# Gates kept as columns and sent through DRAM, LN2 transposed by DMA, attention DMAs issued by GpSimd, and idle products at the start: a fused attention and feed-forward block

## Chip, cores, metric

One core of a Trainium2 chip. The time is the device time of one execution in microseconds (us); most executions agree within 0.3% for the kernel before. Each experiment was timed in the same rounds, on the same chip, as the kernel before. TensorE is PE, VectorE DVE, ScalarE ACT, GpSimd POOL, SyncE SP.

## The reference

A transformer block on 2048 tokens of width 512, conditioned by a vector c: local attention (32 heads of 16, window of 8 keys at a distance of 2), then a SwiGLU feed-forward part (FFN) of width 1792. All arrays are bf16.

```python
mod = (silu(c) @ w_mod).reshape(1, 6, 1, 512)
sa, ca, ga, sb, cb, gb = ...                  # six rows of 512
h = layernorm(x) * (1 + ca) + sa              # LN1
x = x + ga * attention(h, wqkv, wo)           # ga: a gate on the columns of wo
h = layernorm(x) * (1 + cb) + sb              # LN2
x = x + gb * (silu(h @ w1) * (h @ w3)) @ w2   # gb: a gate on the columns of w2
```

The gates ga and gb are multiplied into wo and w2 once, so each gate has to stand in SBUF as a row of 512 that is repeated on all 128 partitions.

## The kernel before

The kernel is a list of operations with a cost in nanoseconds, an engine and a key. A planner inside the program places them: at each moment it takes, for each free engine, the ready operation of lowest priority number. So the order on each engine follows from the costs, the modelled latencies and a table of tuned priorities. The chip then runs each engine's instructions strictly in that order, with semaphore waits between engines.

```python
LAT = {"sp": 1900, "pe": 230, "dve": 70, "act": 150, "pool": 120}
DMA_RATE = 350
...                                     # in schedule(): how long a DMA takes in the plan
                if o.dma:
                    dma_free = max(busy[e], dma_free) + o.bytes // DMA_RATE
                    o.end = dma_free + LAT["sp"]
```

The gate, with silu(c) spread over 128 equal columns beforehand (`csb`), comes out of PE already repeated on all partitions:

```python
    def gate(i):
        def mm(e):
            for t in range(KT):
                ins = e.matmul(bank(vm), csb[:, t, :], wm_g[i][:, t, :], start=(t == 0), stop=(t == KT - 1))
            return ins
        p.op("pe", mm, 4 * MM, k, r=[vwmg[i], vcsb] + wm_hold, w=[vm])
        p.op("act", lambda e: e.activation(dst[:], bank(vm), ACT.Copy), c_act(512), k, r=[vm], w=[vg[i]])
```

LN2 (and LN1) of a tile of 128 tokens: statistics on DVE, two small GpSimd steps for the reciprocal root, normalisation on DVE, four 128x128 transposes on PE, eviction with scale and shift on ACT:

```python
        vn = Val("xn", xnpool)
        p.op("dve", lambda e: e.tensor_scalar(vn.at[:], x_sb[:, T, :], mv[:, i, 0:1], rs[:, i, :], op0=ALU.subtract,
                                              op1=ALU.mult), 350, ("nm", i), r=[vx[T], vr, vm], w=[vn])
...                                     # ln_T
                p.op("pe", tr, 120, k, r=[vns[tt], vident], part=[vt])
```

The attention weights of a tile go to DRAM and come back in another layout, both issued by SP; then DVE multiplies them with the values (`av`, 128x4096) and PE reduces:

```python
        p.dma(bass.AP(a_dram, ...), ..., ("ad", T), 65536, r=[va, ve], w=[vad], cost=400)
        p.dma(lambda: val.at[:], bass.AP(a_dram, ...), ("al", T), 65536 * 3, r=[vad], w=[val], cost=400)
```

The softmax here doesn't subtract the row's maximum and nothing guards it: scores larger than these inputs give would overflow.

Of the kernel before, what the change touches and what calls it, by code (L numbers as in the profile page):

```python
# [11 lines left out]
P = 128  # L12
# [71 lines left out]
class Program:  # L84
# [41 lines left out]
    def dma(self, out, in_, key, nbytes, r=(), w=(), part=(), after=(), eng="sp", cost=450, group=None):  # L126
        nc = self.nc

        def fn(e):
            a = out() if callable(out) else out  # L130
            b = in_() if callable(in_) else in_
            with nc.allow_non_contiguous_dma(reason="layout"):
                return e.dma_start(a, b)

        o = self.op(eng, fn, cost, key, r=r, w=w, part=part, after=after, dma=nbytes)
        if group is not None:
            group.append(o)
            o.group = group
        return o

    def schedule(self, prio):
# [21 lines left out]
        dma_free = 0  # L163
# [3 lines left out]
        while len(self.placed) < len(ops):  # L167
# [10 lines left out]
            for e in ENGINES:  # L178
# [31 lines left out]
                if o.dma:  # L210
                    dma_free = max(busy[e], dma_free) + o.bytes // DMA_RATE
                    o.end = dma_free + LAT["sp"]
                else:
                    o.end = busy[e] + LAT[e]
# [115 lines left out]
VG = 2  # L330
LN1 = [[0, 1], [2, 3], [4, 5, 6, 7], [8, 9, 10, 11], [12, 13, 14, 15]]
# [3 lines left out]
def _build(p, A_x, A_wqkv, A_wo, B_w1, B_w3, B_w2, c, w_mod, out):  # L335
# [37 lines left out]
    cst = sb([P, 2], f32, "cst")  # L373
# [3 lines left out]
    cT = sb([P, KT], bf, "cT")  # L377
    thc = sb([P, KT], f32, "thc")
    csT = sb([P, KT], f32, "csT")
    csT_bf = sb([P, KT], bf, "csT_bf")  # L380
    modc_bf = sb([P, 16], bf, "modc_bf")
    modc = sb([P, 16], f32, "modc")
# [11 lines left out]
    csb = at([P, KT, P], bf, "csb", 24576)  # L394
    zrow = at([PAD, D], bf, "zrow", 25600)
    wm_g = [at([P, KT, 512], bf, f"wm_g{i}", 12288 * i + 8192) for i in range(2)]
    vsh_x = nc.alloc_sbuf_tensor_at("sb_vshx", [P, 8, D], bf, offset=nc.lookup_mloc(wqkv).addr)

    v_dram = nc.dram_tensor("v_scratch_dram", (PAD + S, D), bf)
    a_dram = nc.dram_tensor("a_scratch_dram", (S, W * H), bf)  # L400
# [19 lines left out]
    def held(pool, items):  # L420

        vals = []
        for i, item in enumerate(items):
# [9 lines left out]
    k = ("const", 0)  # L433
    p.op("pool", lambda e: e.memset(ident[:], 0.0), 150, k, w=[vident])
# [3 lines left out]
    p.op("pool", lambda e: e.memset(cst[:, 1:2], -0.5), 80, k, part=[vcst])  # L438
    k = ("const", 1)
    p.op("pool", lambda e: e.memset(ones[:], 1.0), 150, k, w=[vc])  # L440
# [21 lines left out]
    p.dma(bass.AP(cT, 0, [[KT, P], [1, KT]]), bass.AP(c.tensor, c.offset, [[1, P], [P, KT]]), ("load", 0), 1024, w=[vcT],  # L462
          eng="act")
    for T in range(4):
        p.dma(x_sb[:, T, :], x_view[:, T, :], ("load", 1 if T < 2 else 19), 131072, w=[vx[T]])
    p.dma(wm_s[0][:], wm_view[:, :, 0:1024], ("load", 2), 1048576, w=[vwms[0]])
# [20 lines left out]
    for g in range(NG):  # L487
# [10 lines left out]
    vthc, vcs, vcsb, vcsf = Val("thc"), Val("cs"), Val("csb"), Val("csf")  # L498
    k = ("mod", 0)
    p.op("act", lambda e: e.activation(thc[:], cT[:], ACT.Tanh, scale=0.5), 200, k, r=[vcT], w=[vthc], table="exp")  # L500
    p.op("dve", lambda e: e.scalar_tensor_tensor(csT_bf[:], thc[:], 1.0, cT[:], op0=ALU.add, op1=ALU.mult), 180, k,
         r=[vthc, vcT], w=[vcs])
    p.op("dve", lambda e: e.tensor_scalar(csT_bf[:], csT_bf[:], 0.5, None, op0=ALU.mult), 180, k, w=[vcs])
    k = ("mod", 1)
    p.op("dve", lambda e: e.tensor_copy(csT[:], csT_bf[:]), 180, k, r=[vcs], w=[vcsf])
    for t in range(KT):
        p.op("dve", lambda e, t=t: e.tensor_scalar(csb[:, t, :], ones[:], csT[:, t:t + 1], None, op0=ALU.mult), 180, k,
             r=[vc, vcsf], part=[vcsb])
# [4 lines left out]
    def modulation(i):  # L513
# [12 lines left out]
        p.op("pe", mm, 1000, k, r=[vwms[i], vcs] + wm_hold, w=[vm])  # L526
# [4 lines left out]
        p.op("dve", lambda e: e.tensor_copy(modc[:, jlo:jlo + 8], modc_bf[:, jlo:jlo + 8]), 180, k, r=[vb16], w=[vmod[i]])  # L531

    def gate(i):
        k = ("mod", 4 + i)
        vm = Val("ps_gate", psum)

        def mm(e):
            for t in range(KT):
                ins = e.matmul(bank(vm), csb[:, t, :], wm_g[i][:, t, :], start=(t == 0), stop=(t == KT - 1))
            return ins  # L540

        p.op("pe", mm, 4 * MM, k, r=[vwmg[i], vcsb] + wm_hold, w=[vm])
        dst = (ga_bc, gb_bc)[i]
        p.op("act", lambda e: e.activation(dst[:], bank(vm), ACT.Copy), c_act(512), k, r=[vm], w=[vg[i]])

    def ln_stats(which, T):
# [10 lines left out]
        vn = Val("xn", xnpool)  # L557
        p.op("dve", lambda e: e.tensor_scalar(vn.at[:], x_sb[:, T, :], mv[:, i, 0:1], rs[:, i, :], op0=ALU.subtract,  # L558
# [3 lines left out]
    def ln_T(which, gi, vns):  # L562
        vh = Val("h", hpool)
        n = len(vns)
        for half in range(2):
# [12 lines left out]
            for j in range(2):  # L578
# [14 lines left out]
                if half and not which and gi < 2:  # L593
# [121 lines left out]
    def values(T, i, ve, va):  # L715
# [4 lines left out]
              lambda: ve.at[0][:, i].rearrange("p w h -> p (w h)"), ("ad", T), 65536, r=[va, ve], w=[vad], cost=400)  # L720
        p.dma(lambda: val.at[:], bass.AP(a_dram, T * P * W * H, [[H, P], [16 * W * H, 8], [1, H]]), ("al", T), 65536 * 3,
              r=[vad], w=[val], cost=400)
# [41 lines left out]
    def ffn_unit(gi, n, fi, vh):  # L764
# [11 lines left out]
        p.op("pe", lambda e: mm(e, vgp, w1), 4 * c_mm(n), k, r=[vh, vw13[g]], w=[vgp])  # L776
        p.op("act", lambda e: e.activation(vt.at[:, 0:n], bank(vgp)[:, 0:n], ACT.Silu), c_act(n), k, r=[vgp], w=[vt],  # L777
             table="silu")
        p.op("pe", lambda e: mm(e, vup, w3), 4 * c_mm(n), k, r=[vh, vw13[g]], w=[vup])
# [4 lines left out]
    finals = []  # L784

    def ffn_w2(T, tt, vhh):
        vz = Val("ps_z", psum)
        o = None
        for q in range(2):
            def mm(e, q=q):  # L790
# [5 lines left out]
            o = p.op("pe", mm, 7 * MM, ("z", 2 * T + q), r=vhh[7 * q:7 * q + 7] + [vw2s], part=[vz], after=[o] if q else [])  # L796
        vo = Val("o", opool)
        p.op("dve", lambda e: e.tensor_tensor(vo.at[:], bank(vz), x_sb[:, T, :], ALU.add), c_dve(512), ("zo", T),  # L798
             r=[vz, vx[T]], w=[vo])
        finals.append(p.dma(out2d[T * P:(T + 1) * P, :], lambda: vo.at[:], ("zo", T), 131072, r=[vo], cost=400))  # L800

    modulation(0)
# [24 lines left out]
    for gi, Ts in enumerate(FFN):  # L827
        vns = [ln_stats(1, T) for T in Ts]
        vh = ln_T(1, gi, vns)
        vhh = [ffn_unit(gi, len(Ts) * P, fi, vh) for fi in range(NF)]  # L830
        for tt, T in enumerate(Ts):
            ffn_w2(T, tt, vhh)
# [6 lines left out]
def _priorities():  # L839

    return {
        "ac": [-200350, -305143, -144949, -247454, -248998, -144926, 118091, 153034, 127660, 128134, 144119, -511708, -511789, 144159, 233884,
            140161],
        "ad": [-17874, -30405, -32779, -22500, -24840, -32434, -28265, -27668, 1469, -27769, 384, 367, 2705, 132755, -1479, -1613],
        "al": [-26059, -18199, -29495, -32976, -260310, -30646, -28356, -25679, -27023, -29130, 662, 915, 2008, 137184, 1131, 135573],
        "av": [-237126, -167739, 117729, 116760, 129499, 127502, -3576, 163212, 134914, 166331, 224073, 159673, 234283, 170474, 234369, 175760],
        "const": [-318511, -250028],
        "ex": [-152588, -142436, -140021, 53300, -139876, 74900, 96361, 96500, 96599, 118100, 127701, 139700, 124737, 182900, 182900, 182900],
        "f": [-13079, -234848, -103997, -152504, -114086, -145296, -116384, -248184, -248481, -146619, -145234, -198977, 121830, -31495, -146237,
# [61 lines left out]
```

## Time and profile before

| | kernel before |
|---|---|
| time, median | 255.9 us (255.0 to 256.3) |
| profiled execution | span 253.2 us |
| PE busy | 239.0 us, 94% |
| TensorE clock full from | 16.28 us, to the end |

Three more rows of the before page matter; each has 40 slices of the span, here of 6.3 us. PEclk is the granted TensorE clock in tenths (it takes off only what a record of half rate covers; in this trace the first record, full rate, begins at 16.28 us, so the slower start doesn't show in it), DMA the busy share of the 16 DMA engines, GB/s what they moved.

```profile
PEclk9999999999999999999999999999999999999999
DMA  6997999899954595322369145393001000000101
GB/s 193 359 324 189 293 350 331 210 331 284 241 123 140 142 310 196 64 31 62 106 194 295 54 104 85 87 310 103 4 0 44 0 0 21 21 3 21 41 23 41
```

The view of DMA issues (what, how many, size of each, median us from issue to landing):

```profile
v_scratch_dram<-sb_v SPq DMA_DIRECT2D x16, 128.0 KB, 5.0
a_scratch_dram<-sb_attn SPq DMA_DIRECT2D x16, 64.0 KB, 2.5
```

### The profile page before, as it was taken

To read this page: it belongs to the slowest core of one execution; us is meant where nothing else is said; L and a number is where in the kernel's file an instruction comes from. 1 tells how busy PE (TensorE), PEld (TensorE's weight loads), DVE (VectorE), ACT (ScalarE), POOL (GpSimd) and SP (SyncE) were. 2 spreads that over 40 slices of the span, in tenths; PEclk is the share of its full clock that TensorE was granted. 3 is DMA by queue.
4 is the path that set the end of the run, shared out by engine and by line. 5 is a ranking of instruction groups with operands and counts; after the bars stand their busy time and mean duration, and the time that the engine had idled before them with its cause. 6 is when DMAs were issued, how large, how long until landed. Compare 5 with 4: busy or idle time off the path is not lost.

```text
span 253.2 us, 5473 instructions
## 1 busy us (share of the span) xinstructions
PE 239.0 (94%) x2262; PEld 140.4 (55%) x2296; DVE 191.7 (76%) x298; ACT 111.4 (44%) x198; POOL 32.0 (13%) x81
## 2 busy tenths in 40 slices
PE   0599989999999999999999999999999999999995
PEld 0367555655488666546654544556544444565562
DVE  4759889999998989999899899999952443432432
ACT  2159748864863347432462273334234322420120
POOL 6237641001000040000002200020030000000000
PEclk9999999999999999999999999999999999999999
DMA  6997999899954595322369145393001000000101
GB/s 193 359 324 189 293 350 331 210 331 284 241 123 140 142 310 196 64 31 62 106 194 295 54 104 85 87 310 103 4 0 44 0 0 21 21 3 21 41 23 41
DMA packets 45817, 36.29 MB, mean 143 GB/s; under 512 B 19408, under 2 KB 36576, under 8 KB 45792
## 3 DMA queue, kind: packets, MB, share of 16 engines
q1 hardware_dynamic: 45264, 35.94, 49.4%
q8 instruction: 18, 0.29, 0.5%
q10 hardware_dynamic: 528, 0.00, 0.1%
q14 instruction: 7, 0.06, 0.1%
HBM read 30.67 MB, written 5.26 MB: 142 GB/s over the span
## 4 chain that ended last, share of the span: by engine, by line
PE 87%; DVE 5%; DMA 2%; POOL 2%; issue 1%; SPq 0%; ACT 0%; DVEq 0%
PE pall L771 36%; PE pall L792 19%; PE pall L615 9%; PE pall L755 5%; PE pall L742 5%; PE pall L633 5%; PE pall L673 4%; PE pall L574 2%; DMA sb_x<-in_A_x_dram 2%; POOL sb_rs L555 1%; DVE sb_xn L558 1%; DVE sb_st L550 1%; POOL sb_rs L553 1%; DVE sb_pq L664 1%; DVE sb_hh L780 1%
## 5 line engine op out<-in xcount | busy, mean ns | idle before, releaser
L771 PE MATMUL pall<-sb_h,sb_w 128*128 128x512 bf16 (+1 forms) x548 | 100.0, 336 | 0.7
L771 PEld LDWEIGHTS pall<-sb_h,sb_w 128*128 128x128 bf16 x560 | 53.7, 97 | 41.4
L777 ACT ACTIVATE sb_sg<-pall 128x512 bf16<-128x512 f32 (+1 forms) x70 | 35.6, 511 | 70.6 <-PE pall L771 70.3
L780 DVE TENSOR_TENSOR sb_hh<-sb_sg,pall 128x512 bf16<-128x512 bf16 (+1 forms) x70 | 39.5, 577 | 26.0 <-PE pall L771 23.8
L792 PE MATMUL pall<-sb_w,sb_hh 128*128 128x512 bf16 x216 | 49.7, 379 | 0.4
L664 DVE TENSOR_TENSOR sb_pq<-sb_q,sb_kT 128x4096 bf16<-128x4096 bf16 x16 | 36.4, 2283 | 0.5 <-ACT sb_q L622 0.3
L792 PEld LDWEIGHTS pall<-sb_w,sb_hh 128*128 128x128 bf16 x224 | 21.4, 98 | 23.5 <-DVE sb_hh L780 0.2
L615 PE MATMUL pall<-sb_h,sb_wqkv 128*128 128x512 bf16 (+1 forms) x155 | 31.9, 344 | 0.3
L582 ACT ACTIVATE sb_h<-pall,sb_modc 128x512 bf16<-128x512 bf16 (+1 forms) x36 | 23.1, 708 | 18.7 <-PE pall L574 13.1
L553 POOL TENSOR_TENSOR sb_rs<-sb_mv,sb_cst 128x1 f32<-128x1 f32 x32 | 8.8, 276 | 151.4 <-DVE sb_mv L551 148.4
L733 DVE TENSOR_TENSOR sb_vsh<-sb_vsh,sb_al 128x4096 bf16<-128x4096 bf16 x12 | 27.3, 2285 | 0.4 <-DMA sb_vsh<-v_scratch_dram 0.4
L798 DVE TENSOR_TENSOR sb_o<-pall,sb_x 128x512 bf16<-128x512 f32 x16 | 11.0, 688 | 18.0 <-PE pall L792 18.0
L550 DVE BATCH_NORM_STATS2 sb_st<-sb_x 128x6 f32<-128x512 bf16 x32 | 21.8, 682 | 3.3 <-DMA sb_x<-in_A_x_dram 3.2
L555 POOL TENSOR_TENSOR sb_rs<-sb_rs,sb_cst 128x1 f32<-128x1 f32 x32 | 20.9, 654 | 2.5
L615 PEld LDWEIGHTS pall<-sb_h,sb_wqkv 128*128 128x128 bf16 x160 | 15.1, 101 | 11.0 <-ACT sb_h L582 0.7
L633 PE MATMUL pall<-sb_wqkv,sb_h 128*128 128x512 bf16 x63 | 17.6, 411 | 1.5 <-DVE sb_xn L558 1.3
L574 PE MATMUL pall<-sb_ident,sb_xn 128*128 128x128 bf16 x128 | 12.8, 227 | 6.4 <-DVE sb_xn L558 6.4
L673 PEld LDWEIGHTS pall<-sb_E,sb_pq 128*128 128x128 bf16 x512 | 14.7, 96 | 2.7 <-DVE sb_pq L664 0.6
L748 ACT ACTIVATE sb_ot<-pall 128x512 bf16<-128x512 f32 x16 | 9.6, 598 | 13.6 <-PE pall L742 13.6
L574 PEld LDWEIGHTS pall<-sb_ident,sb_xn 128*128 128x128 bf16 x128 | 9.5, 101 | 10.6 <-DVE sb_xn L558 6.9
L755 PE MATMUL pall<-sb_wo,sb_ot 128*128 128x512 bf16 x58 | 15.0, 379 | 0.3
L673 PE MATMUL pall<-sb_E,sb_pq 128*128 128x32 bf16 x512 | 15.1, 177 | 0.0
(59 smaller groups left out, 163.8 us busy)
## 6 DMA issues: line engine op xcount, KB each, us to landing
sb_vsh<-v_scratch_dram SPq DMA_DIRECT2D x48, 256.0 KB, 4.4
sb_vshx<-v_scratch_dram SPq DMA_DIRECT2D x16, 256.0 KB, 4.5
sb_wm_s<-in_w_mod_dram SPq DMA_DIRECT2D x2, 1024.0 KB, 6.6
v_scratch_dram<-sb_v SPq DMA_DIRECT2D x16, 128.0 KB, 5.0
sb_w<-in_B_w_dram SPq DMA_DIRECT2D x4, 512.0 KB, 7.9
out_dram<-sb_o SPq DMA_DIRECT2D x16, 128.0 KB, 1.7
sb_w<-in_B_w_dram SPq DMA_DIRECT2D x1, 1792.0 KB, 8.9
sb_wqkv<-in_A_wqkv_dram SPq DMA_DIRECT2D x3, 512.0 KB, 7.9
```

The source lines that it names most:

```text
L550: o = p.op("dve", lambda e: e.bn_stats(st[:, i, :], x_sb[:, T, :]), 670, k, r=[vx[T]], w=[vs])
L574: ins = e.transpose(b[:, col:col + P], vns[tt].at[:, ft * P:(ft + 1) * P], ident[:])
L615: ins = e.matmul(bank(vp)[:, 0:n], wqkv[:, t, col:col + P], vh.at[:, t, 0:n], start=(t == 0), stop=(t == KT - 1))
L633: ins = e.matmul(bank(vp), vh.at[:, t, tt * P:(tt + 1) * P], wqkv[:, t, 2 * D:3 * D], start=(t == 0), stop=(t == KT - 1))
L664: return e.tensor_tensor(vp.at[:], in0, in1, ALU.mult)
L673: ins = e.matmul(b[:, c0:c0 + H], vp.at[:, w, ft, :], E_sb[:, ft, :], start=(ft == 0), stop=(ft == KT - 1))
L733: return e.tensor_tensor(v_w, v_w, a_w, ALU.mult)
L755: ins = e.matmul(bank(vy), vt.at[:, ft, :], wo[:, ft, :], start=(ft == 0), stop=(ft == KT - 1))
L771: ins = e.matmul(bank(vp)[:, 0:n], wt[:, t, fi * P:(fi + 1) * P], vh.at[:, t, 0:n], start=(t == 0), stop=(t == KT - 1))
L777: p.op("act", lambda e: e.activation(vt.at[:, 0:n], bank(vgp)[:, 0:n], ACT.Silu), c_act(n), k, r=[vgp], w=[vt], table="silu")
L780: p.op("dve", lambda e: e.tensor_tensor(vh_.at[:, 0:n], vt.at[:, 0:n], bank(vup)[:, 0:n], ALU.mult), c_dve(n), k, r=[vt, vup], w=[vh_])
L792: ins = e.matmul(bank(vz), vhh[fi].at[:, tt * P:(tt + 1) * P], w2[:, fi, :], start=(fi == 0), stop=(fi == NF - 1))
```

## The change

The intent: PE is the bound, so take work from it and start it at full clock. Gates are computed as columns (32 products of one column) and turned into repeated rows by a store to DRAM and a broadcast load; LN2's transposes move from PE to the DMA transpose, its normalisation from DVE to ACT; GpSimd issues the attention DMAs; 80 products of ones keep PE busy before and just behind the first modulation; c is loaded in rows; the last two tiles end in column halves. FFN products get extra dependencies on earlier ones, and all priorities are new.

```diff
+    def warm(i, after=()):
+            for _ in range(4):
+                ins = e.matmul(bank(vw)[:, 0:P], ones[:], ones[:], start=True, stop=True)
...
     def gate(i):
-                ins = e.matmul(bank(vm), csb[:, t, :], wm_g[i][:, t, :], start=(t == 0), stop=(t == KT - 1))
+            for j in range(4):
+                for t in range(KT):
+                    ins = e.matmul(b[:, j:j + 1], wm_g[i][:, t, j * P:(j + 1) * P], csT_bf[:, t:t + 1], ...)
...
+        p.op("dve", lambda e: e.tensor_copy(gcol[:, 4 * i:4 * i + 4], bank(vm)[:, 0:4]), 180, k, r=[vm], w=[vgc])
+        p.dma(bass.AP(g_dram, i * D, [[1, P], [P, KT]]), bass.AP(gcol, 4 * i, [[8, P], [1, 4]]), k, 90000, ..., eng="pool", cost=900)
-        p.op("act", lambda e: e.activation(dst[:], bank(vm), ACT.Copy), c_act(512), k, r=[vm], w=[vg[i]])
+        p.dma(dst[:], bass.AP(g_dram, i * D, [[0, P], [1, D]]), k, 131072, r=[vgd], w=[vg[i]], eng="pool", cost=900)
...
     def ln_stats(which, T):
+        if which:                       # nb = -mean * rstd, two more GpSimd steps
+            p.op("act", lambda e: e.activation(vn.at[:], x_sb[:, T, :], ACT.Identity, bias=nb[:, T, :], scale=rs[:, i, :]), ...)
...
     def ln_T(which, gi, vns):
+        if which and gi >= DMA_T:       # DMA_T = 1: all groups but the first
+                p.dma(lambda tt=tt: vh.at[:, :, tt * P:(tt + 1) * P], lambda tt=tt: vns[tt].at[:], k, 157000, ..., transpose=True)
...
-              ..., ("ad", T), 65536, r=[va, ve], w=[vad], cost=400)
+              ..., ("ad", T), 65536, r=[va, ve], w=[vad], cost=900, eng="pool")
...
     # the planner
-                    dma_free = max(busy[e], dma_free) + o.bytes // DMA_RATE
-                    o.end = dma_free + LAT["sp"]
+                    if e == "sp":
+                        dma_free = max(busy[e], dma_free) + o.bytes // DMA_RATE
+                        o.end = dma_free + LAT["sp"]
+                    else:
+                        o.end = busy[e] + 2 * o.bytes // DMA_RATE + LAT["sp"]
```

The store's destination `[[1, P], [P, KT]]` names element p + 128 t for partition p and column t.

## The prediction

> **What bounds the kernel now.** I read the page's busy shares first, then the slices, the chain that ended last, the waits of the TensorE alone, the timeline at both ends, and last the windows.
>
> ```profile
> PE 239.0 (94%) x2262; PEld 140.4 (55%) x2296; DVE 191.7 (76%) x298; ACT 111.4 (44%) x198; POOL 32.0 (13%) x81
> PE   0599989999999999999999999999999999999995
> DVE  4759889999998989999899899999952443432432
> ```
>
> PE is busy everywhere but in the first slices and the last. DVE is full too until about slice 29 (185 us) and then half idle: two engines share the middle, PE alone has the last 70 us. Busy PE is not PE at full rate, so the chain is next (start, length, what):
>
> ```profile
> 10.51 3.59 PE pall L633 x8
> 14.10 0.85 PE pall L615 x4
> 15.16 0.85 PE pall L615 x4
> 16.23 1.40 PE pall L615 x12
> ...
> 192.53 9.93 PE pall L771 x46
> ```
>
> At 192 us a product of 512 columns takes 9.93/46 = 0.216 us; at 10.5 us it took 3.59/8 = 0.449. Four of 256 columns took 0.85 us at 14-15 us and 12 took 1.40 (0.117 each) after 16.2. The full rate comes at about 16.3 us.
>
> Work at full rate, from the program's counts: products of 512 columns 336 (FFN) + 224 (w2) + 96 (q, k) + 64 (v) + 64 (wo) + 8 (gates) = 792 x 0.216 = 171.1 us; 288 of 256 columns x 0.109 (the chain has 48 in 5.24 us at 239 us) = 31.4; 1024 reductions of 32 or 16 columns x 0.025 (64 in 1.59 at 98 us) = 25.6; 64 modulation products likewise 1.6; 128 transposes x 0.056 (8 in 0.45 at 22 us) = 7.2. Sum 236.9. The first product starts at 5.6, the last ends near 250.3, and 2.9 us of eviction and store follow. 253.2 - 236.9 - 5.6 - 2.9 leaves 7.8 us lost between. Where, say the waits of PE (total, times, longest) and the rates above:
>
> ```profile
> PE pall L574 <- DVE sb_xn L558: 6.4, 2, 5.6
> PE pall L522 <- DMA sb_wm_s<-in_w_mod_dram: 1.5, 1, 1.5
> PE pall L633 <- DVE sb_xn L558: 1.3, 1, 1.3
> PE pall L633 <- ACT sb_q L622: 0.2, 1, 0.2
> ```
>
> Nearly all lies before 10.5 us. Two holes of 1.5 and 1.3 us, plus half rate until 16.3, make 1.8 + 1.7 + 2.8 = 6.3 of the 7.8; 1.5 us are spread over the other 237. So removing waits in the middle can bring almost nothing. Only fewer PE products, a better start and a shorter tail can.
>
> **What the Trainium skill says.** "TensorE: Matmul & The Clock Gate", Part 1: the array runs at half clock until it has been busy for about one window of 3.4 us; back to back 427 ns cold, 216 ns warm for 512 columns. The trace agrees (0.449 with its waits, 0.216), and turns 5.8 us after 10.5; the short bursts before did not count as busy.
>
> "SBUF — State Buffer", Who interferes with whom: a VectorE instruction with two SBUF inputs and a GpSimd instruction that reads SBUF block each other. The trace agrees; the same 128x1 power takes 0.55 us elsewhere:
>
> ```profile
> 27.39 2.29 DVE L664 TENSOR_TENSOR sb_pq<-sb_q,sb_kT 128x4096 bf16<-128x4096 bf16 x1 [0.34 <-ACT sb_q L622]
> 27.39 2.70 POOL L555 TENSOR_TENSOR sb_rs<-sb_rs,sb_cst 128x1 f32<-128x1 f32 x1
> ```
>
> "DMA: Bandwidth & Descriptors", Anatomy of one DMA: about 2 us are fixed; here an attention-weight store and its reload need 2.5 us each, so this agrees. The same page, SWDGE vs HWDGE vs iDMA: DMAs issued by GpSimd have their descriptors written by its cores into SBUF, and a transpose must come from SP or ACT. No DMA in this kernel comes from GpSimd, so nothing here shows that cost.
>
> **The change, part by part.**
>
> *Idle products.* 14 x 4 products of ones, 128 columns, with no input but a memset on DVE, can start near 1.3 us. Cold, at 107 ns (half the warm rate), they last 56 x 0.107 = 6.0 us, to about 7.3, so the clock should be full before the modulation (7.76 now), and 6 x 4 more fill the hole behind it (24 x 0.056 = 1.3 us in a gap of 1.56). They lie in idle time and cost nothing. They bring up to 2.8 us. I take 2.4: in the first two groups of two tiles ACT then has about 6.5 us of evictions (8 of 0.39, 2 of 0.60, 4 of 0.56) for 5.7 us of products, the more so as the second group's evictions all move from DVE to ACT.
>
> *c in rows, x in pairs.* c is waited for by the tanh at 3.74, far from the 7.76 of the modulation; its transpose and copy (some 0.4 us) are hidden. The modulation waits for 1 MB of w_mod, issued at 1.71 behind two x loads; one x load less ahead of it saves an issue of 0.43. I take 0.4 us earlier.
>
> *Gates.* 8 x 0.216 = 1.7 us become 32 x 0.027 = 0.9: 0.8 us of PE. Two evictions of 0.6 leave ACT, and four scalings of 0.25 leave DVE. The two trips through DRAM (store, reload, near 5 us plus issue) end long before the first wo product at about 58 us and the first w2 product at 86: hidden.
>
> *LN2 transposes.* 14 of the 16 tiles: 56 x 0.056 = 3.1 us leave PE. On DVE the 16 normalisations leave (16 x 0.40 = 6.5 us), on ACT 16 x 0.6 = 9.6 come, at 44% busy. I estimate each group's way from last residual to h at 9 to 13 us: stats 0.9, four GpSimd steps 1.2 or 3.5 if blocked, ACT 0.65, issue of up to four transposes, landing 2.5 to 4.5, four modulations of 0.6. Now it is 6.5 to 10 (last residual 91.6, last h 98.3; 140.5 to 146.9). Behind it lies the earlier group's w2, 56 x 0.216 = 12 us, and wo and reductions.
>
> *Attention DMAs from GpSimd.* SP is freed of 32 issues of 0.4 to 0.6 us and no longer stands in line at those waits. There is no PE time in it.
>
> *Last two tiles in column halves.* The last eviction falls from 0.69 to 0.42 us and the last store to half: 0.4 us.
>
> Sum: 2.4 + 0.4 + 0.8 + 3.1 + 0.4 = 7.1 us. DVE loses 6.5 + 1.0 + 0.7 = 8 us too, most of it before 185 us, so it can keep up with a PE that is 6 us ahead. That matters, because now a group of four tiles comes out of attention every 45 us (h ready at 98, 147, 189) and PE needs about 46 us for one: they are matched. Against the 7.1 I set 0.6 for new waits. Time before 255.9 - 6.5 = 249.4; since kernels retuned with the change (all priorities are new) usually have their waits smoothed, I go to 249.0.
>
> **Rivals.**
>
> *The transposes' latency becomes a wait.* For: h of the second group is ready at 98.3 and its products run from 99.6 on; no slack is visible there, and each transpose stands in SP's queue between value loads that take 4.4 us to land. Against: w2 of the group before can be held back, the last group has tens of microseconds, and three h buffers are there. If three boundaries lose 2 us each: 255.
>
> *GpSimd becomes the slow link.* It gets 32 DMAs, of which each reload waits in line for its own store, plus 32 more small steps; each read can be held 2.3 us by a VectorE product, and DVE spends 73 us in those (36.4 + 27.3 + 9.1). For: the 2.70 above. Against: 13% busy now, and tiles are fetched several at a time into 5 buffers. If attention slipped by 2 to 4 us per group but DVE's spare 8 us absorbed half: 252 to 254.
>
> *The start doesn't gain.* The first q, k and v weights are DMA-bound (DMA share 1.11 between 10 and 20 us), and DVE, 94% busy from 20 to 180 us, sets the pace: then the 2.4 us are waited off later and the end moves only by what is cut behind 185 us: about 1.5 us of transposes and 0.4 of tail, giving 253 to 254.
>
> *All of it.* No new wait, the full 2.8 and less spread loss: 247.5.
>
> **Range and chances.** The sum's size is well founded, as 236.9 us is counted, so the fast side is tight: below 245.5 something would have to go that I don't see. The slow side holds three rivals of 253 to 255. Range 245.5 to 253.5. The 2% line is 250.8, 1.8 above the estimate: faster 0.73, same 0.23, slower 0.04.
>
> **What would show it.** Right: the granted clock is full before 8 us; the first projections take 0.216 per 512 columns or 0.109 per 256; the start of FFN comes 2 to 3 us earlier; LN2's transposes on PE shrink to 8; after 20 us PE's waits sum below 2 us; the tail is 2.5. Wrong: waits of PE for ACT's h of L582's successor at a group's start (first rival), for GpSimd's DMA through DVE's value products (second), or for weights and DVE's products before 60 us (third). The prediction as a whole fails if PE's waits after 20 us exceed 4 us, or if its products start later than 10.5 us.

## More of the kernel before

For the first 70 us the DMA engines are 60 to over 90% busy and move 190 to 360 GB/s: weights and x. A high busy share goes with a high rate.

## The result

The changed kernel took 283.3 us in the median of four runs (281.0 to 288.4); two of them were slow, the fast ones took 281.43 and 280.96. The ratio to the kernel before, of fast runs, is 1.101 (95% interval 1.093 to 1.109). A ratio here is always the mean time of one kernel's fast runs over that of the other's in the same rounds, so it is not quite the ratio of the medians that are quoted. The prediction, 249.0 with a range of 245.5 to 253.5, was wrong by 32 us (fast runs) and in its sign.

The page of the changed kernel (slices of 7.0 us):

```profile
PEclk9999779799999687999999999999999999999999
DMA  7998299999969699912053596961532100000111
GB/s 236 355 262 25 22 217 352 346 339 302 300 160 117 56 209 177 241 24 57 2 190 69 142 257 136 258 166 30 145 45 74 42 0 2 0 19 0 40 38 38
```

In slices 4 and 5 (21 to 35 us) the DMA engines move 25 and 22 GB/s, a tenth of what the slices beside them move. In slice 4 the busy share is 8 all the same: engines at work that move next to nothing. In slices 13 and 14 (84 to 98 us) it is 117 and 56 GB/s at a share of 9 and 6. (The low rates of slices 18 to 20 are another thing: the share is low there too, little was asked for.) And PEclk, which was 9 throughout before, dips in six slices. The records of the granted clock have half rate from 32.05 to 38.88, 52.53 to 55.94, 93.49 to 100.32 and 107.14 to 110.56 us, 20.5 us in all; before, none between 16.28 us and the end. Each of these stretches begins in or at the end of a hole in PE's work (2.5, 2.5, 5.7 and 3.5 us), so such a hole costs its own length and then part of the next 3.4 or 6.8 us.

What happens at those times, in the timeline (start, length, instructions, in brackets the idle time before and what ended it):

```profile
17.57 0.92 POOL L133 DMA_DIRECT2D g_scratch_dram<-sb_gcol  x1 [1.16 <-DVE sb_gcol L565]
31.57 0.60 ACT L688 ACTIVATE sb_v<-pall 128x512 bf16<-128x512 f32 x1 [5.84 <-DMA v_scratch_dram<-sb_v]
36.80 0.60 POOL L133 DMA_DIRECT2D sb_ga_bc<-g_scratch_dram  x1 [10.87 <-DMA g_scratch_dram<-sb_gcol]
...
82.71 0.80 POOL L133 DMA_DIRECT2D g_scratch_dram<-sb_gcol  x1
87.74 1.28 ACT L822 ACT_TABLE_LOAD   x1
95.18 0.95 ACT L822 ACTIVATE sb_sg<-pall 128x256 bf16<-128x256 f32 x3 [6.15 <-remote]
95.62 5.94 PE L816 MATMUL pall<-sb_h,sb_w 128*128 128x256 bf16 x32 [5.72 <-ACT sb_sg L822]
100.45 0.59 POOL L133 DMA_DIRECT2D sb_gb_bc<-g_scratch_dram  x1 [14.06 <-issue]
109.98 2.03 DVE L885 TENSOR_TENSOR sb_w<-sb_w,sb_gb_bc 128x3584 bf16<-128x3584 bf16 x1 [2.94 <-DMA sb_gb_bc<-g_scratch_dram]
```

The first gate store is issued at 17.57 and its reload goes out at 36.80, 19.2 us later; the second takes from 82.71 to 100.45, 17.7 us. One kilobyte each. No wait of PE names the gates themselves, though DVE stands 2.94 us for the second one before it scales w2. Within both spans others wait: ACT's eviction of v stands 5.84 us for a v store that has to free its buffer, and a Silu of ACT stands 6.15 us for something that the view doesn't name ("remote"); PE then waits for ACT.

The trace's semaphore records tell what "remote" is. A semaphore is a counter that an engine raises when a piece of its work is done, and on which others wait. This Silu waits for PE's semaphore alone. The six last products before PE's stop that raise it ended from 87.7 to 89.9 us; the six raises are recorded only from 95.16 to 95.62, the first of them 7.4 us late, and the Silu starts at 95.18. Elsewhere a raise is recorded about 0.01 us after its product. PE's raises that come more than 0.1 us late are found in the traces of the changed kernel, of e4 (four, up to 6.3 us) and of e12 (seven at the second store, up to 5.8 us), which have the same gate store, and in none of the 16 other traces that can be used. So this store delayed PE's own signals too, and not DMAs alone; by which path, no trace shows.

PE's longest waits (total, times, longest):

```profile
PE pall L816 <- ACT sb_sg L822: 5.9, 2, 5.7
PE pall L787 <- DVE sb_vsh L778: 5.0, 2, 3.5
PE pall L527 <- DMA sb_wm_s<-in_w_mod_dram: 3.3, 2, 2.5
PE pall L678 <- ACT sb_v L688: 2.5, 1, 2.5
```

All of these but 0.7 us of the third line lie after 20 us, the 2.5 of the third among them (the second modulation weights, at 52.5 us). Of the waits that the prediction lists for the kernel before, 0.95 us lay after 20 us. And the DMA issues that answer to those shown before:

```profile
v_scratch_dram<-sb_v SPq DMA_DIRECT2D x16, 128.0 KB, 7.7
a_scratch_dram<-sb_attn POOLq DMA_DIRECT2D x16, 64.0 KB, 4.1
sb_h<-sb_xn SPq DMA_TRANSPOSE x14, 3.1
```

At the start the clock is full from 4.74 us, as predicted. But the first q and k products do not start earlier for it: 11.18 us against 10.51 before, later than the 10.5 us that the prediction named as a sign of failure. They wait for q's weights:

```profile
11.18 1.03 PE L660 MATMUL pall<-sb_h,sb_wqkv 128*128 128x256 bf16 x8 [1.21 <-DMA sb_wqkv<-in_A_wqkv_dram]
```

### The profile page after: what moved, and what is told of

Read it like the earlier page. It is cut to its first block, busy times and chain, and to the rows that moved or that the text cites. A ratio compares the mean times of both kernels' runs of the same rounds, so it can differ in the third digit from the quotient of the medians.

```text
span 279.7 us, 5682 instructions
## 1 busy us (share of the span) xinstructions
PE 248.1 (89%) x2337; PEld 147.2 (53%) x2373; DVE 185.9 (66%) x281; ACT 121.7 (44%) x214; POOL 68.9 (25%) x149
## 4 chain that ended last, share of the span: by engine, by line
PE 47%; DMA 26%; DVE 12%; issue 6%; ACT 4%; POOL 2%; SPq 2%; ACTq 0%; DVEq 0%
PE pall L816 27%; PE pall L852 11%; DMA v_scratch_dram<-sb_v 6%; DVE sb_pq L709 5%; DMA a_scratch_dram<-sb_attn 5%; DMA sb_gb_bc<-g_scratch_dram 3%; DMA sb_h<-sb_xn 3%; DMA sb_wqkv<-in_A_wqkv_dram 3%; DMA g_scratch_dram<-sb_gcol 3%; PE pall L800 2%; DMA sb_al<-a_scratch_dram 2%; PE pall L839 2%; PE pall L787 2%; SPq L133 2%; DVE sb_hh L825 1%
## 5 line engine op out<-in xcount | busy, mean ns | idle before, releaser
L816 PE MATMUL pall<-sb_h,sb_w 128*128 128x512 bf16 (+1 forms) x549 | 102.9, 343 | 8.0 <-ACT sb_sg L822 5.9
L852 PE MATMUL pall<-sb_w,sb_hh 128*128 128x512 bf16 x188 | 43.5, 379 | 1.0 <-DVE sb_hh L825 0.6
L778 DVE TENSOR_TENSOR sb_vsh<-sb_vsh,sb_al 128x4096 bf16<-128x4096 bf16 x14 | 32.0, 2287 | 11.6 <-DMA sb_vsh<-v_scratch_dram 7.0
L577 POOL TENSOR_TENSOR sb_rs<-sb_mv,sb_cst 128x1 f32<-128x1 f32 x32 | 14.6, 455 | 51.5 <-DVE sb_mv L575 49.0
L574 DVE BATCH_NORM_STATS2 sb_st<-sb_x 128x6 f32<-128x512 bf16 x32 | 21.9, 685 | 5.2 <-DMA sb_x<-in_A_x_dram 4.9
L862 DVE TENSOR_TENSOR sb_o<-pall,sb_x 128x512 bf16<-128x512 f32 (+1 forms) x18 | 11.2, 628 | 20.4 <-PE pall L852 15.3
L133 POOL DMA_DIRECT2D sb_al<-a_scratch_dram x16 | 14.4, 901 | 28.5 <-DMA a_scratch_dram<-sb_attn 28.3
L586 ACT ACTIVATE sb_xn<-sb_x,sb_nb,sb_rs 128x512 bf16<-128x512 bf16 x16 | 13.0, 811 | 17.6 <-POOL sb_nb L585 17.6
L787 PE MATMUL pall<-sb_ind,sb_vsh 128*128 128x16 bf16 x448 | 13.3, 169 | 5.0 <-DVE sb_vsh L778 5.0
L787 PEld LDWEIGHTS pall<-sb_ind,sb_vsh 128*128 128x128 bf16 x448 | 13.1, 96 | 8.1 <-issue 3.6
L133 POOL DMA_DIRECT2D a_scratch_dram<-sb_attn x16 | 8.7, 548 | 34.3 <-DVE sb_attn L755 34.3
```

The source lines that it names most:

```text
L133: return e.dma_start(a, b, transpose=True) if transpose else e.dma_start(a, b)
L574: o = p.op("dve", lambda e: e.bn_stats(st[:, i, :], x_sb[:, T, :]), 670, k, r=[vx[T]], w=[vs])
L778: return e.tensor_tensor(v_w, v_w, a_w, ALU.mult)
L787: ins = e.matmul(b[:, ft * P + 16 * g:ft * P + 16 * g + 16], vv.at[:, g, ft * P:(ft + 1) * P], ind[:], start=True, stop=True)
L816: ins = e.matmul(bank(vp)[:, 0:n], wt[:, t, fi * P:(fi + 1) * P], vh.at[:, t, 0:n], start=(t == 0), stop=(t == KT - 1))
L852: ins = e.matmul(bank(vz), vhh[fi].at[:, tt * P:(tt + 1) * P], w2[:, fi, :], start=(fi == 0), stop=(fi == NF - 1))
```

## The experiments

Eighteen kernels. "Order unchanged" means that each engine has its instructions in the order of the kernel that was edited. Letters of theories are labels: A is that the gate stores hold the DMA engines and everything that needs them, D that the DMAs which GpSimd issues cost by themselves, F that the order was planned with durations that are too short. Where another letter stands, the words around it carry the meaning.

| run | what | us | ratio to before |
|---|---|---|---|
| changed kernel | | 283.3 | 1.101 |
| e1_store8 | gate store in pieces of 8 bytes | 268.4 | 1.053 |
| e2_row | gate as one row of 1 KB | 262.7 | 1.034 |
| e3_spread | 2-byte pieces, 512 bytes apart | 263.8 | 1.038 |
| e4_idle_pool | before + two such stores, from GpSimd | 276.3 | 1.084 |
| e12_idle_sp | the same, from SP | 278.5 | 1.093 |
| e5_att_sp | e2, attention DMAs from SP | 272.2 | 1.067 |
| e6_pe_tr | e2, LN2 transposes on PE | 276.5 | 1.084 |
| e7_no_idle | e2 without idle products | 264.4 | 1.038 |
| e8_before_idle | before + idle products | 254.9 | 0.999 |
| e9_before_att_pool | before, attention DMAs from GpSimd | 255.0 | 1.005 |
| e10_row_replanned | e2, order planned anew | 257.6 | 1.011 |
| e11_before_replanned | before, order by the same planner | 262.4 | 1.030 |
| e13_row_plan2 | e2, second search of the order | 255.9 | 1.004 |
| e16_row_plan3 | the same, another start | 260.8 | 1.023 |
| e14_before_plan2 | before, second search | 260.5 | 1.020 |
| e15_pe_tr_plan2 | e13 with LN2 transposes on PE | 262.5 | 1.031 |
| e17_row_wmod_first | e13, first loads in another order | 252.9 | 0.994 |
| e18_short_idle | e17 with idle products cut to 1 column | 253.0 | 0.992 |

All results were correct but e1 and e3, which are wrong. The times are medians of all executions, slow ones too (two of the changed kernel, one each of e4, e14 and e16); the ratios are of fast ones. One execution of e16, the profiled one, took 859 us; it is unexplained, and not used.

### Is it the gate store?

**e1_store8.** Each partition writes its four values side by side; the gates come out permuted.

```diff
-        p.dma(bass.AP(g_dram, i * D, [[1, P], [P, KT]]), ...
+        p.dma(bass.AP(g_dram, i * D, [[4, P], [1, 4]]), ...
```

> The changed kernel with its gate stores as 128 runs of 8 bytes in place of 512 of 2 bytes; the gates come out in a wrong order, on purpose, and the order of every engine is unchanged. Theory A (the 512 two-byte writes hold the DMA rings some 18 us each, and all that waits for a DMA then waits): a quarter of the writes, so 4 to 5 us from issue to landing where the trace of the changed kernel has 19.2 and 17.7, and 250 to 260 us in all. Theory B (DMAs issued from GpSimd are slow to land next to a busy DVE, whatever their shape): landing stays near 18 us, time 278 to 288. Theory C (the LN2 transposes or the attention reloads cost the time, the gates none of it): store lands early, time still over 272.

268.4 us, 1.053 (1.048 to 1.057). Half of the loss is gone with 128 pieces of 8 bytes in place of 512 of 2; store to reload is now 8.7 us (17.5 to 26.2) and 7.7 us. Theory A had expected 4 to 5 us and 250 to 260 in all: right in direction, but the times came out above what it said, here and in the next two runs (247 to 255 and 250 to 260 had been expected).

**e2_row.** The gate as one row on one partition (4 products of 512 columns), stored as one run of 1 KB and then broadcast as before; correct, order unchanged.

```diff
+                ins = e.matmul(b[0:1, :], csT_bf[:, t:t + 1], wm_g[i][:, t, :], start=(t == 0), stop=(t == KT - 1))
+        p.op("dve", lambda e: e.tensor_copy((ga_bc, gb_bc)[i][0:1, :], bank(vm)[0:1, :]), 180, k, r=[vm], w=[vgc])
+        p.dma(bass.AP(g_dram, i * D, [[D, 1], [1, D]]), (ga_bc, gb_bc)[i][0:1, :], k, 90000, ..., eng="pool", cost=900)
```

> The changed kernel with each gate computed as one row of 512 on one partition (4 products of 512 columns), stored as whole pieces and loaded back to 128 partitions as before; still through DRAM and from GpSimd, right result, same order on every engine. Theory A: store lands in 2 to 3 us, PE waits after 20 us fall below 8, time 247 to 255. Theory B: landing still over 10 us, 275 to 288. Theory C: over 272.

262.7 us, 1.034 (1.030 to 1.038). In the ratio, 6.7 of the 10.1 points are gone; only the gate's own product, copy and store were touched. The rate row of its page has no hole left at 21 to 35 us (slices of 6.5 us, numbers 4 to 6):

```profile
GB/s 233 358 284 128 230 363 353 346 318 264 88 111 319 257 274 83 40 23 95 129 181 170 230 114 288 101 30 99 105 27 96 1 0 3 0 20 0 63 20 40
```

**e3_spread.** Still 512 writes of two bytes, but each 512 bytes from the next. The reload reads c in place of the gate, so the result is wrong and no unwritten memory is read.

```diff
-        p.dma(bass.AP(g_dram, i * D, [[1, P], [P, KT]]), ...
+        p.dma(bass.AP(g_dram, i * 256 * D, [[256, P], [256 * P, KT]]), ...
```

> The changed kernel with its 512 two-byte writes spread in DRAM, each 512 bytes from the next (the gates are then loaded from another tensor: wrong result on purpose), same order on every engine. If theory A holds because neighbouring two-byte writes of different DMA rings collide in the same piece of DRAM: landing under 6 us and 250 to 260 us. If it holds because each small write costs its ring a fixed time: landing still 15 to 20 us and 276 to 288. Theory B: as the latter. Theory C: over 272 either way.

263.8 us, 1.038 (1.033 to 1.043), within 1.1 us of the row; the two stores land in 5.3 and 6.0 us. So it isn't the number of small writes. It is that the two-byte pieces lie next to each other in DRAM. That several DMA engines have to take turns at one place is a reading that fits; no run tells pieces of several engines from pieces of one, and the inside of it is not seen in any trace.

**e4_idle_pool.** The kernel before, order unchanged, and beside each gate's product one such store of 512 elements which nobody reads, issued by GpSimd.

```diff
+        finals.append(p.dma(bass.AP(g_dram, i * D, [[1, P], [P, KT]]), bass.AP(ident, 0, [[P, P], [1, 4]]), k, 1,
+                            r=[vident], after=[o], eng="pool", cost=1))
```

> The kernel before, its order on every engine unchanged, plus two stores of 512 two-byte elements to a DRAM tensor that nobody reads, issued by GpSimd after each gate's products (about 19 and 64 us). Theory A: DMA throughput falls under 50 GB/s for 15 us after each, time 265 to 282. Theories B and C: within 2 us of the kernel before, 255 to 258.

276.3 us, 1.084 (1.081 to 1.088): 21.9 us for two kilobytes that no instruction waits for before the end. Its rate row has the hole (the stores go out at 19.1 and 75.2 us, the slices are 6.9 us), and PE's longest waits name ACT. In the first of them ACT's eviction of v stands 9.54 us for a v store; in the second ACT stands 6.53 us for "remote", that is, for raises of PE that come 5.2 to 6.3 us late:

```profile
GB/s 205 359 307 31 0 143 370 360 270 316 292 140 25 41 223 185 299 141 62 14 151 84 265 136 88 99 94 294 81 1 18 22 0 0 19 21 19 36 23 38
```

```profile
PE pall L577 <- ACT sb_v L646: 8.2, 1, 8.2
PE pall L774 <- ACT sb_ot L751: 5.7, 1, 5.7
```

**e12_idle_sp.** The same stores from SP.

```diff
-                            r=[vident], after=[o], eng="pool", cost=1))
+                            r=[vident], after=[o], eng="sp", cost=1))
```

> The kernel before with the two idle stores of 512 two-byte elements (as in the run that took 276.3) issued by SP in place of GpSimd. If the cost is the writes themselves: 268 to 280 again. If it belongs to DMAs whose descriptors GpSimd writes: 255 to 257.

278.5 us, 1.093 (1.086 to 1.099). The issuer doesn't matter beyond a per cent. This fits the Trainium skill ("DMA: Bandwidth & Descriptors", section Issuing engines are not separate DMA queues: DMAs started by any engine run on the same 16 engines and interleave), and this pair of runs agrees. Here a Silu that follows no table load stands 5.94 us for "remote". Theory A is shown from both sides: the stores taken away or spread, and the stores alone added (what they hold up includes PE's signals).

### What is left after the row

e2 is still 3.4% slower than before. In its trace PE loses about 7.6 us around 48 to 61 us and 4 us around 153 to 160, each with a stretch of half clock behind it (54.88 to 61.70 and 157.28 to 160.69). PE's waits and the two chains that lead to them:

```profile
PE pall L787 <- DVE sb_vsh L778: 5.3, 2, 4.3
...
PE pall L800 <- ACT sb_ot L793: 1.4, 1, 1.4
...
PE pall L816 <- ACT sb_h L604: 1.0, 1, 1.0
```

```profile
40.93 0.90 POOL L133 DMA_DIRECT2D sb_al<-a_scratch_dram  x1 [5.88 <-DMA a_scratch_dram<-sb_attn]
...
148.03 2.48 POOL L579 TENSOR_TENSOR sb_rs<-sb_rs,sb_cst 128x1 f32<-128x1 f32 x1
150.98 0.81 ACT L586 ACTIVATE sb_xn<-sb_x,sb_nb,sb_rs 128x512 bf16<-128x512 bf16 x1 [5.27 <-POOL sb_nb L585]
```

First: an attention store from GpSimd, amid weight loads, lands after 5.88 us where the plan had given it 65536 x 2 / 350 + 1900 = 2.3 us. Second: the GpSimd steps of a tile are held by DVE's 128x4096 products (2.48 us for a power of 0.55), then ACT takes 0.81 us to normalise where the plan had 0.6. Is it the issuing engine, one of the moved parts, or the order?

**e5_att_sp.** e2 with the 32 attention DMAs issued by SP, at the same places of the plan.

```diff
         p.schedule(_priorities())
+        for o in p.placed:
+            if o.key[0] in ("ad", "al"):
+                o.eng = "sp"
+        p.order = {e: [o for o in p.placed if o.eng == e] for e in ENGINES}
```

> The row-gate kernel (e2_row, 262.7) with its 32 attention-weight stores and reloads issued by SP at the same points of the schedule; PE, DVE and ACT orders unchanged. Theory D (what is left over the kernel before is the GpSimd issue of these DMAs: a store then a reload landed in about 12 us together at 35 to 47 us, PE waited 4.5 us at 52 us for the value product behind them, and the clock then fell to half for 6.8 us): that wait goes, 254 to 258. Theory E (it is the way of LN2: GpSimd's small steps held by long DVE products, then transposes, a wait of PE at 153 to 157 us): unchanged, 261 to 264. Theory F (the new order of work alone, tuned for other durations, is to blame): also 261 to 264.

272.2 us, 1.067 (1.061 to 1.073), 9.4 us worse, which no theory had expected. SP issues in order, and a reload that waits for its own store to land (19.0 us in all, over ten waits) holds the loads behind it:

```profile
PE pall L794 <- DVE sb_vsh L785: 12.3, 4, 8.1
```

So in this order, planned for GpSimd, the move is needed.

**e9_before_att_pool.** The reverse: before, with the attention DMAs from GpSimd, order unchanged (the same edit with `"pool"`).

> The kernel before with its 32 attention-weight stores and reloads issued by GpSimd at the same points of its schedule; PE, DVE and ACT orders unchanged. Theory D (issuing them from GpSimd costs time by itself): 258 or more, with waits of DVE's value products for the reload. Theory F (only an order of work planned for shorter landings suffers): within 2 us of the kernel before, as its order leaves 7 us and more between a store and the product that needs it.

255.0 us, 1.005 (0.998 to 1.012). Thirty-two DMAs from GpSimd cost nothing that this run can resolve. Theory D falls, in the order of the kernel before.

**e6_pe_tr.** e2 with LN2's transposes back on PE.

```diff
-DMA_T = 1
+DMA_T = 9
```

> The row-gate kernel with all LN2 transposes on PE again (normalisation still on ACT); the order after the first FFN products is planned anew. Theory E: the waits at 153 to 157 us go, 256 to 260, though PE gets 3.1 us of transposes back. Theory D: no gain, 263 to 266, as the wait at 52 us comes earlier than any LN2 transpose. Theory F: anything, since the order moves.

276.5 us, 1.084 (1.080 to 1.088). This doesn't tell what LN2 is worth: with other operations and unchanged priorities the planner gave another order everywhere. Inconclusive for its purpose, but even with 3.1 us of PE taken off for the transposes, some 10 us remain; that they belong to an order that nobody tuned is likely, not shown.

**e7_no_idle and e8_before_idle.** The idle products out of e2, and into the kernel before (order unchanged).

```diff
-NWARM = 14          # e7: and no six groups behind the first modulation
+NWARM = 0
```

```diff
+    for i in range(14): # e8, in the kernel before
+        warm(i)
+    first = modulation(0)
+    for i in range(6):
+        warm(14 + i, [first])
```

> The row-gate kernel without its 80 idle products, all other orders unchanged. If they brought what the prediction said: the granted clock turns full only near 16 us, the first projections run at half rate and the time rises by 2 to 3 us, to 264.5 to 266. If the gain of the start is waited off before 60 us (the third rival of the prediction): within 0.7 us of 262.7.

> The kernel before with the 80 idle products at the head of PE (56 before its first transpose, 24 after the modulation), all other orders unchanged. By the prediction's sum 2.4 us are gained: 251.5 to 253. If DVE or the weight loads pace the first 60 us: 254 to 255, no gain.

e7: 264.4 us, 1.038 (1.031 to 1.045), against e2's 1.034 (1.030 to 1.038); the intervals overlap. e8: 254.9 us, 0.999 (0.997 to 1.002). In e8 the clock is full early and the first products run twice as fast, yet at 40 us PE is only some 0.6 us ahead of the kernel before, and 0.25 at its last product; it waits 0.65 us for weights at 15.3 and 0.82 us for DVE's normalisation at 37.0. In e8 the idle products bring nothing; e7's 1.7 us over e2 lie between its two forecasts, and its spread leaves room for the predicted gain as for none.

**e10_row_replanned and its control e11_before_replanned.** The planner gets durations as measured: GpSimd's DMAs in the shared DMA queue and 1000 ns longer, all DMAs 300 ns longer, gate DMAs 6000 ns, ACT's normalisation 220 ns longer, GpSimd's small steps held by DVE's long products. A search then looks for new priorities. e10 has e2's operations, e11 those of the kernel before.

```diff
-                    else:
-                        o.end = busy[e] + 2 * o.bytes // DMA_RATE + LAT["sp"]
+                    else:
+                        dma_free = max(busy[e], dma_free) + o.bytes // DMA_RATE
+                        o.end = dma_free + LAT["sp"] + (1000 if e == "pool" else 0) + 300
```

> The row-gate kernel with the same operations, but its order of work planned anew with durations taken from the traces: DMAs from GpSimd queue behind SP's loads (in the change they do not), GpSimd steps wait for long DVE products, the ACT normalisation 0.81 us in place of 0.60, and priorities searched again for that. Theory F (what is left is the plan's wrong durations): PE's waits after 20 us fall below 5 us and the time to 250 to 255. Theories D and E (the parts themselves cost time): 258 or more whatever the order.

> Control for the run with the new plan: the kernel before, its operations unchanged, with its order planned by the same durations and the same search. If the new plan alone is what helps, this gains as much as the row-gate kernel does; I expect 253 to 258, no clear change, since its own order lost only 1.5 us after 20 us.

e10: 257.6 us, 1.011 (1.006 to 1.017); e11: 262.4 us, 1.030 (1.024 to 1.034). With the same operations, another order gains 5.1 us: theory F is supported, though e10 falls between its forecast (250 to 255) and that of the rivals (258 or more). And under the same planner the changed operations come out 4.8 us under the old ones. That the old operations take 7 us longer in this order than in the one they came with says how well the latter had been tuned.

### How far do comparisons of plans carry, and what is LN2 worth?

The search was made once more, alike for three sets of operations; it now judges a plan by how long it lasts when transfers land up to 1.5 us late and ACT, DVE and GpSimd take up to 2% longer. The edits are the priorities, and for e15 `DMA_T = 9`.

> The operations of e10 (gates as rows), order searched anew so that it bears transfers up to 1.5 us late; planned length 250.3 us. Theory F (the rest of the loss is the order, planned with too short durations): 252 to 256 us, below e10 (257.6) and at or below the kernel before (255.4). If the changed operations themselves cost more than before (rival), it stays at 257 or more.

> The same operations as e13, another start of the search; planned length 252.9 us. It tells the chance of the search: 2 to 3 us over e13 if the planned length carries to the chip, else within 1 us; more than 5 us apart would mean that no comparison of two plans here tells anything.

> Control: the operations of the kernel before through the same search; planned length 253.2 us. Theory F with the changed operations faster by 2 to 5 us: 255 to 260, and e13 under it by 2 to 5. Rival (the difference e10 to e11 was the chance of one search): within 1 us of e13.

> e13's operations with all LN2 transposes on TensorE (56 more transposes of 0.056 us, 3.1 us of PE), through the same search; planned length 253.9 us. If LN2 by DMA is worth what it takes from PE: 2 to 4 us over e13. If the DMA transposes' way costs as much as it saves (first rival of the prediction): within 1 us of e13 or under it.

e13: 255.9 us, 1.004 (1.000 to 1.008). e16, the same operations from another start: 260.8 us, 1.023 (1.021 to 1.025). e14: 260.5 us, 1.020 (1.014 to 1.027). e15: 262.5 us, 1.031 (1.028 to 1.034).

e13 and e16 lie 4.9 us apart with the same operations, as much as e13 and e14 with different ones. So a single pair of plans doesn't tell what operations are worth at this size, and the 4.8 us between e10 and e11 have to be read with that. Over both searches the changed operations have 257.6, 255.9 and 260.8, the old ones 262.4 and 260.5: better on the whole, by an amount that isn't settled. The same holds for LN2: e15 is the slowest, 6.6 us over e13 where 2 to 4 were expected; that is the side on which its 3.1 us more of PE lie, but 1.7 us from e16 is no proof. What e13 does show is that the transposes by DMA need cost no wait: from 60 us on PE loses 0.6 us in the whole rest. (Lost means: the distance between two starts beyond the time of the product at full rate.)

### A version that beats both

e13's loss lies at its start: the first modulation weights land only at 9.6 us, PE has a hole of 2.2 us (its longest wait), and the clock is at half rate from 8.50 to 15.33 us.

```profile
PE pall L536 <- DMA sb_wm_s<-in_w_mod_dram: 2.7, 2, 2.2
```

**e17_row_wmod_first.** e13 with these weights issued one place earlier, ahead of the second pair of x tiles, and one load of four x tiles behind q's weights.

```diff
         p.schedule(_priorities())
+            first = q[:6]               # q = SP's order
+            wm = next(o for o in first if o.key == ("load", 2))
+            new = [first[0], wm] + the rest, its places 3 and 4 exchanged
```

> e13 with the first modulation weights issued before the second pair of x tiles, and one load of four x tiles behind that of q's weights; nothing else moved. If e13's start holds it up: the weights land by about 8.5 us, the half rate is gone or shorter, and the time is 1 to 2.5 us below e13's 255.9, 253.5 to 255, so at or just below the kernel before. If weights and VectorE pace the first 40 us anyway (third rival of the prediction): within 0.7 us of e13.

252.9 us, 0.994 (0.990 to 0.998): in the medians 3 us less than e13, by the ratios 2.5, and 0.6% under the kernel before, a gain clear of noise but under the 2% from which a run here counts as faster. PE's hole ahead of the first modulation is down from 2.2 to 1.7 us and now waits for DVE's normalisation, not for the weights (the 0.7 below is the second modulation, at 47.2 us); the first q and k products start at 13.15 us in place of 13.88, and half rate lasts only from 10.45 to 13.87:

```profile
PE pall L642 <- DVE sb_xn L612: 1.7, 1, 1.7
PE pall L568 <- DVE sb_ones L462: 1.1, 1, 1.1
PE pall L550 <- DMA sb_wm_s<-in_w_mod_dram: 0.7, 1, 0.7
```

The gain was larger than expected (1 to 2.5 us), and here the start does count.

**e18_short_idle.** So the question of the idle products was asked again, in this order: each of the 20 groups of four products of 128 columns becomes one product of one column.

```diff
-            for _ in range(4):
-                ins = e.matmul(bank(vw)[:, 0:P], ones[:], ones[:], start=True, stop=True)
+            ins = e.matmul(bank(vw)[:, 0:1], ones[:], ones[:, 0:1], start=True, stop=True)
```

> e17 with each of the 20 groups of four idle products of 128 columns cut to one of one column; order unchanged. If the idle products bring what the prediction gave them: 1 to 2.5 us over e17's 252.9, and the granted clock not full before 15 us. If they don't count (as e7 and e8 had it): within 0.7 us of e17, or under it, for they hold PE beside the first transposes at half rate.

253.0 us, 0.992 (0.990 to 0.995), the same as e17, although the clock is now full only from 15.12 us. The first q and k products start at 12.85 us here and at 13.15 in e17: what precedes them is c, x and the modulation weights, not PE.

```profile
5.84 0.18 PE L534 MATMUL pall<-sb_ident,sb_c4s 4*128 4x4 bf16 x1 [4.21 <-DVE sb_c4s L532]
8.99 0.61 PE L641 MATMUL pall<-sb_ident,sb_xn 128*128 128x128 bf16 x4 [2.85 <-DVE sb_xn L611]
12.85 2.58 PE L682 MATMUL pall<-sb_h,sb_wqkv 128*128 128x256 bf16 x12 [0.40 <-DVE sb_h L656]
```

So in two orders (e8, e18) the idle products bring no gain, and in the third (e7) none that can be told from noise.

## Why the prediction was wrong

**The step that failed** is in the part on gates: the two trips through DRAM, "store, reload, near 5 us plus issue", were called hidden. The size was wrong (store to reload alone took 19.2 and 17.7 us, against 5 for both), and so was the question. The prediction asked only who waits for the gates, and indeed no PE work stood for them for long. It did not ask what the store does to everything else. While a store of 512 neighbouring two-byte pieces was under way, other transfers nearly stopped (22 to 25 GB/s at the first) and PE's own signals came up to 7.4 us late. At the first store v landed late in DRAM, so ACT got no buffer and PE no bank of PSUM, its result memory (2.5 us of wait); at the second ACT did not learn that PE's products were done, and PE stood 5.7 us for it. The holes also took the granted clock. Taking it away is worth 6.7 of the 10.1 points (e2); adding it alone to the kernel before costs 8.4 (e4). None of the four rivals named it.

**The planner's new times for GpSimd's DMAs** were in the diff and were read as a detail. They give an attention store 2.3 us and the new trip no share of the DMA queue; measured were 4.1 in the median and 5.88 where it hurt (e2). That kernels retuned with the change "usually have their waits smoothed" was an assumption without a line of profile behind it: the order had been smoothed for durations that the chip doesn't have. With the gates mended, another order took 5 to 7 us off the rest (e10, e13). That this is all of the 3.4 points is supported, not shown: the search's own chance is 4.9 us.

**Idle products, 2.4 us:** the clock did what was predicted (full at 4.74 us), the time did not. (The modulation starts 0.3 us earlier, 7.45 against 7.76, near the 0.4 that c and x were to bring; it was lost again in the wait for q's weights.) The third rival, that the start doesn't gain, was right for them (e8, e18). Of its two reasons, weights that come late show in the changed kernel (1.21 us at 11.18). But that the start doesn't count is not so: it does (e17), and it hangs on the order of the first loads.

**LN2 transposes, 3.1 us of PE:** counted rightly, for e2's products are 233.6 us of work at full rate without the idle ones, against 236.6 before, measured from the distances between starts. (A row of 512 columns brings no gain in PE time for the gates, so the difference is LN2's. The 0.8 us for the gates' own products was right too: in the changed kernel the first 16 take 0.40 us at 16.52.) The first rival, their latency as a wait, happened once in the changed kernel: 5.76 us of a transpose's landing are on the page's chain at 167 us, and PE then waits 1.4 and 1.2 us for ACT at 175 and 178. It did not happen in e13. (The chain at 151 us in e2 runs through GpSimd and ACT, not through the transposes.) The ACT normalisation was put at 0.6 us and took 0.81.

**The tail, 0.4 us:** right. From the start of the last product to the end of the span it was 3.28 us before and is 2.90 in the changed kernel.

**GpSimd as the slow link** (second rival): no by itself (e9). But both of its ways appeared in e2: DVE's value product stands 4.75 us for a reload at 54.28 us and PE 4.3 us behind it, and GpSimd's steps held by DVE's products are in the chain at 148 us, 2.48 us for a power.

**What would have shown it wrong:** PE's waits after 20 us above 4 us (they were 23.4), or products that start after 10.5 us (11.18). Both tests worked. The final e17 is 2.0 us shorter in span than the kernel before (251.2 against 253.2), with 3.0 us less work on PE.

## What to carry to other kernels

Before a small DMA is called hidden, look at the size of its pieces and at where neighbouring pieces come from, and ask what it does to every other transfer in flight; a column per partition stored to consecutive addresses was the worst of the forms tried here, and a row from one partition, or the pieces spread out, avoids it. A wait that the profile calls "remote" can be a signal under way: compare when the work ended with when its semaphore was raised. An experiment that adds the suspect alone to the good kernel, with nobody waiting for it, settles such a question in one run. Where an order is planned from modelled durations, compare operations only under plans of like quality, and make two plans of each before you believe a difference of a few per cent.

## What the Trainium skill lacked or had wrong

- "DMA: Bandwidth & Descriptors", Specifications, says that below 512 bytes the DMA engines read, modify and write, and names 512 bytes as the least for full rate. It has nothing on small pieces that lie side by side: 512 writes of 2 bytes to one kilobyte took 19.2 and 17.7 us from store to reload, and at the first the traffic fell to 22 to 25 GB/s where over 200 were moved before and after (two such stores cost e4 21.9 us); the same 512 writes, 512 bytes apart, landed in 5.3 to 6.0 us. Being under 512 bytes was therefore not by itself the cost.
- The same page's fixed cost of about 2 us for a DMA (Anatomy of one DMA, written for DMAs that GpSimd issues) is near the 2.5 us that the attention stores, issued by SP, took in the median before. From GpSimd they took 4.1 us in the changed kernel and, in one case under weight loads, 5.88 us in e2; the row stores of 1 KB took 7.2 and 4.8 us from issue to the issue of the reload. The cost was not constant here.
- No page says that DMA traffic can hold back the signals of a compute engine. While the second gate store was under way, six raises of PE's semaphore were recorded 5.7 to 7.4 us after their products in the changed kernel, four 5.2 to 6.3 us in e4, where nothing depends on the store; ACT, and then PE, stood for them.
